# Block-local attention and a noisy top-2 mixture of experts: the rows of x stored once in token order, 16 bytes scattered per token and expert, rows gathered per tile

## The chip, the core and the metric

The kernel runs on one core of a Trainium2 chip. The metric is the device time of one execution in microseconds (us). Five engines work side by side, each through its own instructions in order: TensorE (PE; its weight loads are listed as PEld), VectorE (DVE), ScalarE (ACT), GpSimd (POOL) and SyncE (SP), which here issues plain DMA transfers. POOL issues the indirect ones, whose rows are picked by a list of indices. A wait of one instruction holds up all that stands behind it on the same engine.

## The reference, cut to what matters

```python
# attention in chunks of 64 tokens; q, k, v: (8, 8, 576, 64)
scores = scale * np.matmul(q_c, k_c.transpose(0, 1, 2, 4, 3))
scores = scores - np.max(scores, axis=-1, keepdims=True)
attn = np.exp(scores)
attn = attn / (np.sum(attn, axis=-1, keepdims=True) + 1e-09)
out = np.matmul(attn, v_c)
...
x = attn_out.transpose(0, 2, 1, 3).reshape(B * S, H * D)      # 4608 tokens x 512
noisy_logits = x @ w_gate + np.log1p(np.exp(x @ w_noise)) * noise
top2 = np.argpartition(-noisy_logits, 2, axis=1)[:, :2]       # 2 of 8 experts
...
    h = np.maximum(x[mask] @ w1[e], 0.0)                      # 512 -> 1024
    out[mask] += top2_w[mask, k, None] * (h @ w2[e])          # 1024 -> 512
```

Every token goes through small attention blocks, then through the two experts with the largest noisy logits, and the two results are added with softmax weights.

## The kernel before, in words

**Attention** (`attend`, L593) takes 36 tiles of 128 tokens, one tile a call, as a pipeline over several calls. In call `it` PE makes the scores of tile `it` (L355), the product with v of tile `it-2` (L381), four transposes of the probabilities of tile `it-1` (L371), four transposes of x of tile `it-3` (L396) and the gate logits of tile `it-4` (L409). A product of q and k covers 64 rows of depth for each of two heads: k is kept with zeros in the other head's rows (`KB`, L308), so that 128 rows and 64 columns of the array give the scores of two heads in one matmul of 128 columns; v is kept likewise (`VB`, L309). So a tile's k and v come as two half transfers of 64 partitions each, q as one whole (L317 to L327): five transfers of SP a tile. The scores of tile t lie in PSUM bank t % 2. DVE takes a row maximum (L359), subtracts it (L364), adds 1e-9 to the row sums (L385), takes reciprocals (L388) and writes x (L391); ACT does the exponential and copies out of PSUM.

**Routing** (`route`, L413) goes over six groups of 4 or 8 tiles (L141). It is a generator whose small DVE steps are put between those of attention (`step_route`), and gives each token two slots: a slot belongs to an expert and a place in its list. **Scatter** (L521): for each tile and each of the two choices, POOL copies one number into `spacer` (L528, L530; that paces it by mx, rc or hh) and issues an indirect DMA (L532) which writes 128 rows of 515 numbers, x and three words on token and weights, into the DRAM table `slots`. 72 of these are spread over attention and the first expert block.

**The experts** are taken in 24 blocks of up to 448 rows, three blocks an expert, expert 0 first and the others in the order of their load (L129). A block's first layer is 8 steps f of 12 matmuls, its second 3 or 4 tiles k of 8 steps f of 3 matmuls; every product is split into three of high and low parts (`three`, L256). Blocks 0, 1 and 2 are expert 0. Their rows are loaded by plain transfers out of `slots` (L202) and turned by PE (L246); blocks 0 and 1 are loaded as soon as routing groups 2 and 4 have been scattered (`EARLY`, L137). Later blocks are loaded from `slots` by four transfers a tile (L207), whose rows the chip picks by the expert's number in a register of SP, and turned by DVE (L250). `x_tile` (L237) turns one tile; its place in the order is written out by hand (`TURNS`, L665, and `hook1`, `hook2_f`). `resolve` (L175) makes row numbers and weights of the words in `slots`. The results are added into `out` by indirect DMAs of POOL (L230). `out` is cleared by 37 transfers of SP (L591) while block 0 runs.

The order of all instructions is the order of the code; nothing is rearranged.

Of the kernel before, what the change touches and what calls it, by code (L numbers as in the profile page):

```python
# [19 lines left out]
P = 128  # L20
# [13 lines left out]
ROW = 576  # L34
CODE, WA, WB, USED = DM, DM + 1, DM + 2, DM + 3
CLEAN = max(CAPS) - P
# [17 lines left out]
def kernel(ctx, tc, qT, kT, vh, wgn, noise, w1, w2, out, caps=CAPS):  # L54
# [36 lines left out]
    nc.vector.memset(caprow[:, 0:1], float(caps[0]))  # L91
    run8 = consts.tile([P, NE], FT, name="run8")
# [44 lines left out]
    EARLY = {0: 2, 1: 4}  # L137
# [58 lines left out]
    def gather_tile(i, k):  # L196
        e, b = BL[i]
        j, r = blocks[e][b][k]
        n = rot["xg"] = rot["xg"] + (i >= NPE)
        x = XG[e, j] = (later_xg[0] if n % 8 in (1, 2, 3) and i >= NPE else xg).tile([P, DM], FT, name="xg")  # L200
        if i < NPE:
            d = nc.sync.dma_start(x[0:r], by_slot[j * P:j * P + r, 0, 0:DM])  # L202
            if i in EARLY:
                early_loads.append(d)
            return
        for q in range(4):
            nc.sync.dma_start(x[32 * q:32 * q + 32, 0:4 * r].rearrange("p (t c) -> p t c", c=P),  # L207
                              by_slot[j * P:j * P + r, ds(place[e], 1), q * P:(q + 1) * P]
                              .rearrange("(t p) o c -> p t (o c)", p=32))

    def gather(i):
        for k in range(len(blocks[BL[i][0]][BL[i][1]])):
            gather_tile(i, k)


    later = [(i, k) for i in range(4, NBL) for k in range(len(blocks[BL[i][0]][BL[i][1]]))]

    ahead = [len(blocks[1][0])]

    def gather_more(most):  # L220
        for _ in range(most):
            if later and ahead[0] < LEAD:
                gather_tile(*later.pop(0))
                ahead[0] += 1
# [40 lines left out]
    def layer1(i, hook, hook_d=lambda f, d: None):  # L265
        e, b = BL[i]
        n = sum(r for _, r in blocks[e][b])
        HT[i] = BH[0 if i == 1 else i % 2]
# [32 lines left out]
    last_rows = ExitStack()  # L301
    rows = last_rows.enter_context(tc.tile_pool(name="rows", bufs=5, side="right"))
    gx = pa.enter_context(tc.tile_pool(name="gx", bufs=2, side="right"))
    work = pv_pools.enter_context(tc.tile_pool(name="work", bufs=3, side="right"))
    vs = pv_pools.enter_context(tc.tile_pool(name="vs", bufs=1, side="right"))
    loads = pk.enter_context(tc.tile_pool(name="loads", bufs=1))
    RING = 6
    KB = [loads.tile([P, 2, 4, P], FT, name=f"kb{n}") for n in range(RING)]  # L308
    VB = [vs.tile([P, 2, 2, 4, 65], FT, name=f"vb{n}") for n in range(RING)]  # L309
    QB = {}  # L310
    HALF = (slice(0, 64), slice(64, 128))
    for n in range(RING):
        for t in (KB[n], VB[n]):
            for h in range(2):
                (nc.vector if n < 2 else nc.gpsimd).memset(t[HALF[1 - h], h], 0.0)

    def load_qk(t):  # L317
        if t < NT:
            QB[t] = loads.tile([P, 4, P], FT, name="qb", bufs=RING)
            nc.sync.dma_start(QB[t], qT[:, t])  # L320
            for h in range(2):
                nc.sync.dma_start(KB[t % RING][HALF[h], h], kT[HALF[h], t])  # L322

    def load_v(t):
        if t < NT:
            for h in range(2):
                nc.sync.dma_start(VB[t % RING][HALF[h], h], vh[HALF[h], t])  # L327

    nc.scalar.preload_act_table_set("natural_log_exp_and_others")
    for j in range(5):  # L330
        load_qk(j)
        if j:
            load_v(j - 1)
# [5 lines left out]
    zero = consts.tile([P, USED], FT, name="zero")  # L339
    nc.gpsimd.memset(zero, 0.0)  # L340

    PR, PT, XS, XT, RC = {}, {}, {}, {}, {}
    by_head = lambda a: a.rearrange("p (g k) -> p g k", k=64)
    sco = [by_head(PS[:, b, :]) for b in range(2)]

    def x_at(t):
        u, r = divmod(t, 4)
        if r == 0:
            XS[u] = rows.tile([P, 4, 520], FT, name="xs")
        return XS[u][:, r]  # L350

    def scores(t):
        for hp in range(4):
            for s in HALF:
                nc.tensor.matmul(PS[s, t % 2, hp * P:(hp + 1) * P], QB[t][:, hp, s], KB[t % RING][:, :, hp, s], start=True, stop=True)  # L355

    def soft_max(t):
        mx = work.tile([P, 8], FT, name="mx", bufs=2)
        nc.vector.tensor_reduce(mx, sco[t % 2], AX.X, OP.max)  # L359
        return mx  # L360

    def soft_sub(t, mx):
        PR[t] = work.tile([P, 512], FT, name="pr")
        nc.vector.tensor_tensor(by_head(PR[t]), sco[t % 2], mx[:, :, None].to_broadcast([P, 8, 64]), OP.subtract)  # L364
# [12 lines left out]
    def pv(t):  # L377
        for hp in range(4):
            for c, s in enumerate(HALF):
                o = 130 * (hp % 2)  # L380
                nc.tensor.matmul(PS[s, 3 + hp // 2, o:o + 130], PT[t][:, hp, s], VB[t % RING][:, :, c, hp, :], start=True, stop=True)  # L381
# [8 lines left out]
    def norm_c(t):  # L390
        nc.vector.tensor_tensor(x_at(t)[:, 0:DM].rearrange("p (b g k) -> p b g k", b=2, k=64), pvb[:, :, :, 0:64], RC[t].to_broadcast([P, 2, 4, 64]), OP.mult)  # L391
# [6 lines left out]
    def x_copy(t):  # L398
        XT[t] = gx.tile([P, ND, P], FT, name="xt")
        nc.scalar.activation(XT[t].rearrange("p d n -> p (d n)"), PS[:, 5, :], AF.Copy)  # L400

    def lg_at(t, n=1):
# [485 lines left out]
```

## Time and profile before

| what | before |
|---|---|
| median of 3 runs | 1029.89 us (1028.78 to 1033.22) |
| the profiled execution | 1029.36 us |
| its span, first to last instruction | 1027.6 us |
| PE busy | 983.1 us (96%) |
| DVE, ACT, POOL busy | 446.1, 271.3, 227.4 us |
| mean granted clock of PE | 0.991 |
| DMA traffic | 132.93 MB, mean 129 GB/s |

The span is what the trace covers; the profiled execution's time is 1.8 us longer. "Busy" counts the time in which at least one instruction of the engine ran. A DMA share of 1.0 means that all 16 DMA engines of the core were busy; it is worked out from packets and comes out slightly above 1 where they overlap. Line numbers L... are those of the kernel before.

### The profile page before, as it was taken

To read this page: it belongs to the slowest core of one execution; us is meant where nothing else is said; L and a number is where in the kernel's file an instruction comes from. 1 tells how busy PE (TensorE), PEld (TensorE's weight loads), DVE (VectorE), ACT (ScalarE), POOL (GpSimd) and SP (SyncE) were. 2 spreads that over 40 slices of the span, in tenths; PEclk is the share of its full clock that TensorE was granted. 3 is DMA by queue.
4 is the path that set the end of the run, shared out by engine and by line. 5 is a ranking of instruction groups with operands and counts; after the bars stand their busy time and mean duration, and the time that the engine had idled before them with its cause. 6 is when DMAs were issued, how large, how long until landed. Compare 5 with 4: busy or idle time off the path is not lost.

```text
span 1027.6 us, 16132 instructions
## 1 busy us (share of the span) xinstructions
PE 983.1 (96%) x5962; PEld 883.5 (86%) x5962; DVE 446.1 (43%) x1005; ACT 271.3 (26%) x542; POOL 227.4 (22%) x332
## 2 busy tenths in 40 slices
PE   6889998999799999999999999999999999999996
PEld 6778887898689889888988998899889998999884
DVE  6656665522525443344334432453245324533311
ACT  3434443211314121222222321232123212322100
POOL 3034754751020111111111102101211111101112
PEclk9999999999899999999999999999999999999998
DMA  8899999864561552264225422553244324412213
GB/s 226 259 292 298 328 323 396 310 177 121 88 166 56 124 117 37 60 140 116 40 46 138 124 40 44 125 135 59 36 121 123 74 43 126 120 21 32 31 21 43
DMA packets 103218, 132.93 MB, mean 129 GB/s; under 512 B 22848, under 2 KB 56000, under 8 KB 103136
## 3 DMA queue, kind: packets, MB, share of 16 engines
q1 hardware_dynamic: 86704, 93.54, 30.4%
q0 software_dynamic: 16432, 38.33, 19.1%
q8 instruction: 48, 0.79, 0.3%
q14 instruction: 34, 0.28, 0.1%
HBM read 81.69 MB, written 50.13 MB: 128 GB/s over the span
## 4 chain that ended last, share of the span: by engine, by line
PE 84%; SPq 6%; DMA 5%; DVE 2%; issue 2%; ACT 1%; POOL 0%; DVEq 0%; ACTq 0%; POOLq 0%
PE PS L263 78%; DMA kb<-in_kT 2%; PE PS L381 2%; SPq L322 1%; PE PS L355 1%; SPq L327 1%; DMA xg<-slots 1%; DMA vb<-in_vh 1%; SPq L207 1%; PE PS L409 1%; PE PS L371 1%; SPq L320 1%; DMA out<-zero 1%; PE PS L396 1%; SPq L107 0%
## 5 line engine op out<-in xcount | busy, mean ns | idle before, releaser
L263 PE MATMUL PS<-xh,w1h 128*128 128x384 f32 (+2 forms) x768 | 262.6, 342 | 9.4 <-DVE hl L277 6.2
L230 POOL DMA_INDIRECT out<-o,lid x77 | 119.3, 1549 | 684.5 <-DVE o L283 680.3
L263 PE MATMUL PS<-xh,w1l 128*128 128x384 f32 (+2 forms) x768 | 261.7, 341 | 0.0
L263 PE MATMUL PS<-xl,w1h 128*128 128x384 f32 (+2 forms) x768 | 261.6, 341 | 0.0
L263 PE MATMUL PS<-w2h,hh 128*128 128x512 f32 x616 | 240.5, 390 | 0.0
L263 PE MATMUL PS<-w2h,hl 128*128 128x512 f32 x616 | 240.2, 390 | 0.0
L263 PE MATMUL PS<-w2l,hh 128*128 128x512 f32 x616 | 240.2, 390 | 0.0
L276 ACT ACTIVATE hh<-PS 128x384 fp32r<-128x384 f32 (+2 forms) x192 | 95.0, 496 | 481.0 <-PE PS L263 425.4
L277 DVE SCALAR_TENSOR_TENSOR hl<-PS,hh 128x384 fp32r<-128x384 f32 (+2 forms) x192 | 108.5, 566 | 188.4 <-ACT hh L276 185.5
L283 DVE TENSOR_SCALAR o<-PS,lwt 128x512 f32<-128x512 f32 x77 | 57.7, 749 | 248.6 <-PE PS L263 246.2
L263 PEld LDWEIGHTS PS<-xh,w1h 128*128 128x128 f32 x768 | 145.3, 189 | 12.7 <-DVE hl L277 6.6
L263 PEld LDWEIGHTS PS<-xl,w1h 128*128 128x128 f32 x768 | 145.4, 189 | 1.9
L263 PEld LDWEIGHTS PS<-xh,w1l 128*128 128x128 f32 x768 | 145.2, 189 | 1.1
L263 PEld LDWEIGHTS PS<-w2h,hl 128*128 128x128 f32 x616 | 112.9, 183 | 27.2
L263 PEld LDWEIGHTS PS<-w2l,hh 128*128 128x128 f32 x616 | 112.9, 183 | 26.2
L263 PEld LDWEIGHTS PS<-w2h,hh 128*128 128x128 f32 x616 | 112.9, 183 | 25.8
L532 POOL DMA_INDIRECT slots<-xs,lii x72 | 72.5, 1007 | 26.5 <-issue 20.8
L253 ACT ACTIVATE xh<-y 128x512 fp32r<-128x512 f32 x67 | 41.2, 614 | 105.5 <-DVE y L250 105.5
L254 DVE TENSOR_TENSOR xl<-y,xh 128x512 fp32r<-128x512 f32 x67 | 44.9, 670 | 47.9 <-ACT xh L253 47.2
L355 PE MATMUL PS<-kb,qb 128*64 128x128 f32 x576 | 40.9, 285 | 13.3 <-DMA kb<-in_kT 12.6
L250 DVE STREAM_TRANSPOSE y<-xg 128x512 f32<-128x512 f32 x67 | 45.6, 681 | 11.9 <-DMA xg<-slots 11.9
L381 PE MATMUL PS<-vb,pts 128*64 128x130 f32 x576 | 39.8, 278 | 9.3 <-ACT xt L400 5.6
(114 smaller groups left out, 686.7 us busy)
## 6 DMA issues: line engine op xcount, KB each, us to landing
st<-in_w SPq DMA_DIRECT2D x64, 512.0 KB
xg<-slots SPq DMA_DIRECT2D x252, 64.0 KB
out<-zero SPq DMA_DIRECT2D x37, 256.0 KB
vb<-in_vh SPq DMA_DIRECT2D x72, 130.0 KB
qb<-in_qT SPq DMA_DIRECT2D x36, 256.0 KB
kb<-in_kT SPq DMA_DIRECT2D x72, 128.0 KB
xg<-slots SPq DMA_DIRECT2D x9, 256.0 KB
slots<-zero SPq DMA_DIRECT2D x8, 257.5 KB
```

The lines of the kernel that those rows point to most:

```text
L207: nc.sync.dma_start(x[32 * q:32 * q + 32, 0:4 * r].rearrange("p (t c) -> p t c", c=P), by_slot[j * P:j * P + r, ds(place[e], 1), q * P:(q ...
L230: s = nc.gpsimd.indirect_dma_start(out=out, out_offset=bass.IndirectOffsetOnAxis(ap=rows_of(i, j)[0:r], axis=0), in_=o[0:r], in_offset=Non ...
L250: nc.vector.transpose(y[:, 0:4 * r], x[:, 0:4 * r])
L253: nc.scalar.activation(oh, src, AF.Copy)
L254: nc.vector.tensor_sub(ol, src, oh.bitcast(FT))
L263: nc.tensor.matmul(p, a, b, start=first and n == 0, stop=last and n == 2)
L276: nc.scalar.activation(hh[:, 0:n], p, AF.Relu)
L277: nc.vector.scalar_tensor_tensor(hl[:, 0:n], p, 0.0, hh[:, 0:n].bitcast(FT), op0=OP.max, op1=OP.subtract)
L283: nc.vector.tensor_scalar(o[0:r], p[0:r], weights_of(i, j)[0:r], None, op0=OP.mult)
L355: nc.tensor.matmul(PS[s, t % 2, hp * P:(hp + 1) * P], QB[t][:, hp, s], KB[t % RING][:, :, hp, s], start=True, stop=True)
L381: nc.tensor.matmul(PS[s, 3 + hp // 2, o:o + 130], PT[t][:, hp, s], VB[t % RING][:, :, c, hp, :], start=True, stop=True)
L532: s = nc.gpsimd.indirect_dma_start(out=slots, out_offset=bass.IndirectOffsetOnAxis(ap=lii[:, k, t0 + r:t0 + r + 1], axis=0), in_=XS[(t0 + ...
```

## The change

x is written once, in token order, to a DRAM table `xbuf`: one plain transfer of SP for each 4 tiles. The scatter writes only 16 bytes per token and choice (`mt`: token and expert code, two weights) into `slots`, still by 72 indirect DMAs of 128 rows. For a tile of an expert's list POOL now gathers 128 rows of `xbuf` by an indirect DMA, after `resolve` has made their numbers: for blocks 0 to 2 straight into the tile that PE turns; for later blocks into a buffer `xr`, from which SP writes the tile to DRAM (`save`) and then loads it with the same four transfers as before (`load_tile`). Rows are fetched 6 tiles and loaded up to 7 tiles ahead. Block 2 becomes an early block too, bound to routing group 5, the last. The zeros that were written to `slots` are fewer.

Attention loads q, k and v as whole transfers of 128 partitions for two tiles at a time, 18 of each. The zero halves are gone: scores and the product with v are matmuls on quarters of the array (64 rows and 64 columns), 16 of each a tile in place of 8, each with half the columns. The scores of a tile take half of two PSUM banks, the same two for every tile, where two tiles took turns. The gate logits are made for 4 tiles at a time: 4 matmuls of 512 columns on column strips of 32, a copy (`gate_copy`), and a sum over the strips one call later (`gate_sum`), so that routing of a group starts one call later and the pipeline has one more call at its end.

The core of the diff:

```diff
-    slots = dram.tile([LROWS * NE, ROW], FT, name="slots")
+    xbuf = dram.tile([NROWS, DM], FT, name="xbuf")
+    slots = dram.tile([LROWS * NE, 4], FT, name="slots")
+    sorted_x = [[dram.tile([P, DM], FT, name=f"x{e}_{j}") for j in range(NLIST)] for e in range(NE)]
-    EARLY = {0: 2, 1: 4}
+    FETCH = 6
+    EARLY = {0: 2, 1: 4, 2: 5}
+    def save(keep=0):
+        while len(unsaved) > keep:
+            e, j, r, x = unsaved.pop(0)
+            nc.sync.dma_start(sorted_x[e][j][0:r], x[0:r])
+    def fetch_tile(i, k):
+        save(1)
...
+            nc.gpsimd.indirect_dma_start(
+                out=x[0:r], out_offset=None, in_=xbuf,
+                in_offset=bass.IndirectOffsetOnAxis(ap=rows_of(i, j)[0:r], axis=0))
+            unsaved.append((e, j, r, x))
+    def load_k(j):
+        kb[j] = loads.tile([P, 2, 4, P], FT, name="kb")
+        nc.sync.dma_start(kb[j], kT[:, 2 * j:2 * j + 2])
     def scores(t):
         for hp in range(4):
-            for s in HALF:
-                nc.tensor.matmul(PS[s, t % 2, hp * P:(hp + 1) * P], QB[t][:, hp, s], KB[t % RING][:, :, hp, s], start=True, stop=True)
+            for h, c in HC:
+                r, s = slice(h * 64, h * 64 + 64), slice(c * 64, c * 64 + 64)
+                o = 64 * hp
+                nc.tensor.matmul(PS[s, h, o:o + 64], q[r, t % 2, hp, s], k[r, t % 2, hp, s], start=True, stop=True)
-                in_=XS[(t0 + r) // 4][:, r % 4, 0:USED], in_offset=None)
+                in_=mt[:, t0 + r, :], in_offset=None)
+                    waiting.append((i, turn[0] + 2))
+    def finish_waiting():
+        while waiting:
+            i = waiting.pop(0)[0]
+            resolve_early(i)
+            gather(i)
+            if (it - 2) % 4 == 3:
+                u = (it - 2) // 4
+                nc.sync.dma_start(xbuf[P + 4 * u * P:P + (4 * u + 4) * P].rearrange("(a p) c -> p a c", p=P), XS[u])
+            if i == 1 and f == 2:
+                finish_waiting()                       # layer 1 of block 1
+            if i == 0 and (k, f) == (0, 4):
+                finish_waiting()                       # layer 2 of block 0
-            if f % 2 == 0:
+            if f % 3:
                 scatter(1)
+            if i == 1 and (k, f) == (0, 5):
+                resolve_all()
+                while len(to_fetch) > len(later) - FETCH:
+                    fetch_tile(*to_fetch.pop(0))
+                gather_more(1)
```

How it moves instructions, at three places. First PE in attention, one call of `attend` before (out<-in, then the size of what is written):

```order
L355 MATMUL PS<-kb_142,qb 64x128 x8
L381 MATMUL PS<-vb_146,pts 64x130 x8
L371 MATMUL PS<-ident,pr 128x128 x4
L396 MATMUL PS<-ident,xs 128x128 x4
L409 MATMUL PS<-wg,xt 128x16 x4
```

and two calls of the change, the second and third after a fourth tile:

```order
L384 MATMUL PS<-kb,qp 64x64 x16
L411 MATMUL PS<-vb,pts 64x65 x16
L400 MATMUL PS<-ident,pr 128x128 x4
L439 MATMUL PS<-xt,wg 32x512 x4
L427 MATMUL PS<-ident,xs 128x128 x4
L452 MATMUL PS<-sel,ls 128x16 x4
```

These are the kinds of rows; the first three and L427 stand in every call, L439 in one call of four and L452 in the next one. The counts of scores and of products with v have doubled with half the columns, and the gate's four matmuls a tile have become eight for four tiles.

Second, POOL at the start of block 0's second layer, where L530 and L528 each stand ahead of a scatter (L532). Before, the kinds of rows there are

```order
L530 COPY spacer<-hh_2258 1x1
L532 DMA slots<-xs,lii 44032x576
L528 MEMSET spacer 1x1
L229 MEMSET spacer 1x1
L230 DMA out<-o,lid_111 4736x512
```

with 16 scatters behind hh in block 0's first layer, 4 behind a memset, then the first store into `out`. In the change they are

```order
L569 COPY spacer<-hh_2696 1x1
L571 DMA slots<-mt,lii 44032x4
L567 MEMSET spacer 1x1
L212 MEMSET spacer 1x1
L216 DMA xg<-xbuf,lid_197 128x512
L257 MEMSET spacer 1x1
L258 DMA out<-o,lid_196 4736x512
```

with 16 scatters behind hh, 2 behind a memset, then the three gathers of block 1 (L212 and L216), three scatters, the first store, five scatters, the second store, the last four scatters, the third store, and then the gathers of block 2. Before, block 1's rows were loaded by SP; now they stand behind 18 scatters on POOL.

Third, DVE in block 1's first layer. Before, eight steps hl follow each other. In the change the last three of these rows, the first of nine that make row numbers for block 2, stand behind the third of them (meta_207 is what SP has loaded of block 2's 16-byte entries):

```order
L305 SCALAR_TENSOR_TENSOR hl_3097<-PS,hh_3096 128x384
L305 SCALAR_TENSOR_TENSOR hl_3099<-PS,hh_3098 128x384
L188 TENSOR_SCALAR rsa<-meta_207 128x4
L189 TENSOR_SCALAR rsb<-meta_207 128x4
L593 TENSOR_SCALAR rsk<-slot_157,lim_204 128x4
```

So the steps hl from the fourth on now stand behind a DMA that itself waits for the last scatter.

More of the change, by code (lines that the diff above doesn't have):

```diff
@@ L194 @@
     early_loads = []
-    def gather_tile(i, k):
+    unsaved = []
+    def save(keep=0):
[4 more added lines that the diff above has]
+        save(1)
         e, b = BL[i]
         j, r = blocks[e][b][k]
-        n = rot["xg"] = rot["xg"] + (i >= NPE)
-        x = XG[e, j] = (later_xg[0] if n % 8 in (1, 2, 3) and i >= NPE else xg).tile([P, DM], FT, name="xg")
+        nc.gpsimd.memset(spacer, 0.0)
@@ L201, in gather_tile @@
         if i < NPE:
[L202 to L205, printed above, removed]
+            last = sum(groups[EARLY[i]])
+            x = XG[e, j] = xg.tile([P, DM], FT, name="xg")
+            nc.gpsimd.indirect_dma_start(
+                out=x[0:r], out_offset=None, in_=xbuf[0:P + last * P, :],
+                in_offset=bass.IndirectOffsetOnAxis(ap=rows_of(i, j)[0:r], axis=0))
+        else:
+            x = later_xg[1].tile([P, DM], FT, name="xr")
+            nc.gpsimd.indirect_dma_start(
+                out=x[0:r], out_offset=None, in_=xbuf,
+                in_offset=bass.IndirectOffsetOnAxis(ap=rows_of(i, j)[0:r], axis=0))
+            unsaved.append((e, j, r, x))
@@ L211, in gather @@
     def gather(i):
         for k in range(len(blocks[BL[i][0]][BL[i][1]])):
-            gather_tile(i, k)
-    later = [(i, k) for i in range(4, NBL) for k in range(len(blocks[BL[i][0]][BL[i][1]]))]
-    ahead = [len(blocks[1][0])]
+            fetch_tile(i, k)
+    later = [(i, k) for i in range(NPE, NBL) for k in range(len(blocks[BL[i][0]][BL[i][1]]))]
+    to_fetch = list(later)
+    ahead = [0]
     def gather_more(most):
+        save()
         for _ in range(most):
+            if to_fetch and len(later) - len(to_fetch) < FETCH:
+                fetch_tile(*to_fetch.pop(0))
@@ L337 @@
     nc.sync.dma_start(nz, noise)
-    zero = consts.tile([P, USED], FT, name="zero")
+    zero = consts.tile([P, DM], FT, name="zero")
     nc.gpsimd.memset(zero, 0.0)
+    mt = consts.tile([P, NT, 4], FT, name="mt")
+    nc.gpsimd.memset(mt, 0.0)
+    load_q(3)
+    load_k(3)
+    load_v(3)
     PR, PT, XS, XT, RC = {}, {}, {}, {}, {}
-    by_head = lambda a: a.rearrange("p (g k) -> p g k", k=64)
-    sco = [by_head(PS[:, b, :]) for b in range(2)]
+    sco = PS[:, 0:2, 0:256].rearrange("p h (g k) -> p h g k", k=64)
+    by_head = lambda a: a.rearrange("p (g h k) -> p h g k", g=4, h=2)
+    HC = [(h, c) for h in range(2) for c in range(2)]
     def x_at(t):
@@ L377, in pv @@
     def pv(t):
+        v = vb[t // 2]
         for hp in range(4):
[L379 to L381 removed]
+            for h, c in HC:
+                r, s = slice(h * 64, h * 64 + 64), slice(c * 64, c * 64 + 64)
+                nc.tensor.matmul(PS[s, 3 + h, hp * 65:hp * 65 + 65], PT[t][r, hp, s], v[r, t % 2, c, hp, :],
+                                 start=True, stop=True)
     def norm_a(t):
@@ L426, in route @@
         ts = slice(t0, t0 + G)
-        parts = [(XS[t0 // 4 + a], slice(4 * a, 4 * a + 4)) for a in range(G // 4)]
         nc.scalar.activation(y, lg[:, :, 1, :], AF.Abs)
@@ L594, in attend @@
         STEPS = 2
-        if it > 0:
-            load_qk(it + 4)
-            load_v(it + 3)
-        if it in (5, 7):
-            for r in range(CLEAN + 64 * (it // 2 - 2), CLEAN + 64 * (it // 2 - 1), 16):
-                nc.sync.dma_start(slots[r * NE:(r + 16) * NE, 0:USED], zero)
-        if it == 7:
-            nc.sync.dma_start(slots[(CLEAN + P) * NE:NLIST * P * NE, CODE:USED].rearrange("(p r) c -> p r c", p=P),
-                              zero[:, 0:3 * (NLIST * P - CLEAN - P) // 16].rearrange("p (r c) -> p r c", c=3))
+        if it % 2 == 0 and it >= 2 and it // 2 + 3 < NT // 2:
+            load_q(it // 2 + 3)
+            load_k(it // 2 + 3)
+        if it % 2 == 1 and it >= 3 and (it - 3) // 2 + 4 < NT // 2:
+            load_v((it - 3) // 2 + 4)
+        if it == 5:
+            nc.sync.dma_start(slots[0:NLIST * P * NE].rearrange("(p r) c -> p (r c)", p=P), zero[:, 0:NLIST * NE * 4])
+            nc.sync.dma_start(xbuf[0:P], zero)
+        turn[0] = it
+        if waiting and it >= waiting[0][1]:
+            finish_waiting()
         if it in (12, 14, 16, 18):
@@ L665 @@
     TURNS = (((1, 1), (1, 5), (2, 1)), ((0, 6), (1, 2), (1, 6), (2, 2)))
-    tail = [NT + 2 + a for a in range(2)]
+    tail = [NT + 2 + a for a in range(3)]
     def hook_tail(f, d):
```

167 lines of the change are left out of this document (87 added, 80 removed).

## Prediction

> **What bounds the kernel now.** I read the windows first, one row for each stage, because the shares of the whole span mix attention with the experts. The columns are the length, the busy time of PE, its weight loads, DVE, ACT and POOL with the instructions in brackets, then PE's granted clock, the DMA share and GB/s.
>
> ```profile
> core 0: us, PE busy (x) PEld busy (x) DVE busy (x) ACT busy (x) POOL busy (x), PEclk, DMA share, GB/s
> 0.00:158.00 158.00, 135.27 (x1678) 123.66 (x1678) 102.65 (x371) 66.56 (x141) 66.75 (x115) 0.99 0.94 289
> 51.00:87.00 36.00, 31.59 (x397) 28.98 (x399) 21.79 (x84) 13.29 (x29) 9.91 (x18) 1.00 0.98 282
> 87.00:124.00 37.00, 32.38 (x393) 29.55 (x389) 25.62 (x103) 18.98 (x44) 26.46 (x38) 0.95 1.03 326
> 154.00:184.00 30.00, 24.30 (x210) 22.42 (x209) 17.77 (x88) 12.58 (x28) 15.15 (x25) 1.00 1.05 396
> 266.00:1018.00 752.00, 751.37 (x3744) 672.89 (x3744) 302.18 (x498) 180.03 (x350) 110.98 (x140) 1.00 0.38 82
> ```
>
> From 266 to 1018 us PE is busy for 751.37 of 752 us. Nothing the change does to x can shorten that stretch: its matmuls stay. What can be won lies ahead of 266 us. In attention (to 158 us) the DMA share is 0.94 and PE is busy for 135 of 158 us; neither is full by itself, so the next view is the chain that ended last, in attention's middle:
>
> ```profile
> 66.69 7.50 DMA kb<-in_kT
> 74.19 0.91 issue
> 75.09 1.09 PE PS L355 x16
> 76.19 0.89 PE PS L381 x16
> 77.07 0.58 PE PS L371 x4
> 77.66 0.44 PE PS L396 x4
> 78.09 0.80 PE PS L409 x8
> 79.12 1.02 PE PS L355 x16
> ```
>
> The chain is a load of k for 7.50 us, then some calls of `attend` at PE's own pace: 1.09 + 0.89 + 0.58 + 0.44 + 0.80 = 3.80 us of matmuls a tile. The real pace comes from PE's timeline, by the first scores and those of the last tile, number 35:
>
> ```profile
> 5.52 3.43 PE L355 MATMUL PS<-kb,qb 128*64 128x128 f32 x32 [5.52 <-DMA kb<-in_kT]
> ...
> 154.00 1.09 PE L355 MATMUL PS<-kb,qb 128*64 128x128 f32 x16
> ```
>
> (154.00 - 5.52) / 35 = 4.24 us a tile, 0.44 above PE's. So attention is bound by transfers that come late, with PE close behind. To gain much, the change has to relieve both, and it does touch both.
>
> **Attention, PE.** A chain row counts 16 instructions for 8 matmuls. L396's four take 0.44 us on the whole array, 110 ns for 128 columns; L381's sixteen, also of 128 columns and on half the array, take 0.89 us, 56 ns each. So two halves already run side by side. Quarters of half the columns would be four abreast at 55 ns, eight groups a phase: 0.45 us for each of scores and product with v, if that goes on. L409's eight instructions take 100 ns each for only 16 columns, so a matmul can have a floor near 0.10 us; with that floor for each group of four a phase takes 0.80. The gate costs 0.11 (four strips abreast, 512 columns at the rate of L396) to 0.44 (one after the other), plus 0.10 for a quarter of the sums: 0.2 to 0.55 a tile, I take 0.5. Scores take 1.02 where the product with v takes 0.89; half of that difference stays, 0.08 with rounding. PE then needs 0.53 + 0.45 + 0.58 + 0.44 + 0.5 = 2.5 us a tile, or 3.2 with the floor. TensorEngine Tiling (Array Packing) of the Trainium skill, under Instruction Overhead, speaks against the change: each matmul carries about 60 cycles, and a factor should not be taken from a dimension already small; L409's row agrees that short ones don't scale, and by an estimate of 25 ns a matmul 32 of them take 0.8 us a phase. Both values lie below the DMA's, next, so this choice doesn't move the sum.
>
> **Attention, DVE.** It is busy for 102.65 us over 36 tiles, 2.85 us each. All scores now use the same banks, so a tile's scores wait for the subtraction (L364) of the tile before: two passes over 512 columns behind 0.53 us of scores, about 2.1 us, which hides under the DMA's pace. If transfers became free, DVE would end the last scores at 5.5 + 36 x 2.85 = 108 us.
>
> **Attention, bytes.** The sizes of the transfers and the count of the scatters in attention:
>
> ```profile
> vb<-in_vh SPq DMA_DIRECT2D x72, 130.0 KB
> qb<-in_qT SPq DMA_DIRECT2D x36, 256.0 KB
> kb<-in_kT SPq DMA_DIRECT2D x72, 128.0 KB
> ...
> slots<-zero SPq DMA_DIRECT2D x8, 257.5 KB
> ...
> L530 POOL COPY spacer<-rc 1x1 f32<-1x1 f32 x23 | 4.1, 178 | 43.0 <-DVE rc L388 39.9 <-issue 1.1 <-DVE goh L458 0.9
> L530 POOL COPY spacer<-mx 1x1 f32<-1x1 f32 x21 | 3.7, 178 | 29.8 <-DVE mx L359 24.5 <-DVE gsp L444 4.1 <-DVE goh L458 0.6
> ```
>
> The first window moved 158 x 289 = 45.7 MB. Loads of q, k, v are 36 x 772 KB = 28.5 MB and stay. The 23 + 21 = 44 scatters of 128 rows of 515 numbers are 11.6 MB and go, the zeros of `slots` are 2.1 MB and nearly go; the plain stores of x come in their place, some 8 MB by the last scores. That leaves 45.7 - 11.6 - 2.1 + 8 = 40 MB. At 282 GB/s (51 to 87 us, loads for the most part) they take 142 us, at 326 (87 to 124, many scatters) 123 us, at 396 (154 to 184, mostly writes) 101 us. The mix after the change lies between the first two windows; I take their mean, 304, which gives 132 us, and shave it to 130 for half as many, longer transfers. Last scores at 130 instead of 154: **-24 us**, between -12 (142) and -44 (110, DVE's bound). DMA: Bandwidth & Descriptors of the Trainium skill, under its rules for kernel authors, says that transfers to disjoint partition halves share the same 16 engines, so whole ones would carry no more bytes a second; DMA shares of 0.98 and 1.03 with halves agree, and by it the time is that of the first bound or my value without the shaving. SP issues three transfers for two tiles where it issued ten; that is slack on SP, not time. The tail from the last scores to the experts keeps its work; the call more and the gate's later sum replace other steps there: 0, within 2.
>
> **Block 1's rows, behind POOL.** PE's timeline at the start of block 0's second layer and of block 1's first:
>
> ```profile
> 192.39 0.39 PE L263 MATMUL PS<-w2h,hh 128*128 128x512 f32 x1
> 192.62 0.40 PE L263 MATMUL PS<-w2l,hh 128*128 128x512 f32 x1
> ...
> 210.20 0.33 PE L263 MATMUL PS<-xh,w1h 128*128 128x384 f32 x1
> ```
>
> POOL's timeline around the start of that layer:
>
> ```profile
> 190.67 0.99 POOL L532 DMA_INDIRECT slots<-xs,lii  x1 [0.16 <-issue]
> ...
> 196.84 0.98 POOL L532 DMA_INDIRECT slots<-xs,lii  x1 [0.16 <-issue]
> 197.82 0.09 POOL L528 MEMSET spacer<- 1x1 f32 x1
> 198.12 0.97 POOL L532 DMA_INDIRECT slots<-xs,lii  x1 [0.22 <-issue]
> 199.09 0.09 POOL L528 MEMSET spacer<- 1x1 f32 x1
> ```
>
> and SP's load of block 1, released by the scatter of 190.67:
>
> ```profile
> 193.45 1.36 SPq L202 DMA_DIRECT2D xg<-slots  x3
> ```
>
> POOL does a scatter in 1.27 us (197.82 to 199.09), and that is the time of its instruction, not of its bytes: I keep it for 16 bytes and for a gather. Its 16th scatter behind hh ends at 197.82, 5.4 us after the second layer begins. Two more scatters (2.6), the first gather (1.3) and a landing (that scatter ended at 191.66, SP went on at 193.45: 1.8) put the first rows 11.1 us into that layer. PE is to turn them after ten steps of three matmuls at 0.23 us, 6.9 us in. PE stands for 4.2 us, and a little more as the other two gathers follow at 1.3 us: **+5**. Were a gather cheaper than a scatter or POOL's queue empty earlier, 0; with slower gathers 9.
>
> **Block 2's numbers, in front of hl.** In block 1's first layer DVE waits, behind the third hl, for the words of the last scatter. On POOL after the 18th scatter (8.0 us into block 0's second layer) come 3 gathers, 12 scatters and two stores, the store's price being
>
> ```profile
> L230 POOL DMA_INDIRECT out<-o,lid x77 | 119.3, 1549 | 684.5 <-DVE o L283 680.3
> L229 POOL MEMSET spacer<- 1x1 f32 x77 | 45.6, 592 | 0.0
> ```
>
> 1.549 + 0.592 = 2.14 us: 8.0 + 15 x 1.3 + 2 x 2.14 = 31.8, and 4 us more to land and load. DVE is there at 17.8 (192.39 to 210.20) + 5 (the wait above) + three steps of 12 x 0.17 = 2.1 us: 29. It stands 7 us, and hl of the next steps and the turned tiles of block 2 queue behind it; PE has free banks for two to three steps, some 5 us, less what DVE then must catch up: **+4**, from 0 (POOL ahead of time) to 10.
>
> **The start of later tiles.** DVE waits 11.92 us for the first later tile and PE 6.18:
>
> ```profile
> 263.50 0.71 DVE L250 STREAM_TRANSPOSE y<-xg 128x512 f32<-128x512 f32 x1 [11.92 <-DMA xg<-slots]
> 266.19 0.74 PE L263 MATMUL PS<-xh,w1h 128*128 128x448 f32 x1 [6.18 <-DVE hl L277]
> ```
>
> This wait goes, since block 2's rows and numbers come earlier and block 3's tiles are fetched from block 1 on. But a chain of six gathers through three buffers, saves and loads is what is late next; its first tile costs about a gather, a landing, a save and a load, some 8 us at 2 us each, and six of them are hidden only if POOL is not behind. -6 + 2 = **-4**, from -6 to +2.
>
> **The rest.** From 266 us fewer gathers than the 77 stores of L230, at 1.3 us, bring POOL from 111 to at most 211 of 752 us. Saves and gathers add at most 77 x 2 x 256 KB = 40 MB to 62 MB, a share of 0.38 to about 0.63. `save` waits on SP for a gather, and weights and tile loads queue behind it; tiles come up to 7 ahead, some 40 us of matmuls, which hides it: 0. With that cover gone, each late tile would cost PE some 2 us.
>
> Sum: -24 + 5 + 4 - 4 = -19. The profiled execution took 1029.36 us, 0.5 below the median of the runs; 1029.4 - 19 = **1010 us**.
>
> **The rivals.** *Quarters one after the other.* If four quarter matmuls don't overlap, a phase is 32 x 56 ns = 1.78 us, PE needs 1.86 + 1.78 + 0.58 + 0.44 + 0.5 = 5.2 us a tile, the last scores are at 5.5 + 35 x 5.2 = 187, 33 later than now: 1029 + 33 + 5 = 1067. It decides from 1.3 us a phase on, where PE is slower than now. The halves that overlap today speak against it, L409's floor speaks for it: 0.07. *No gain in transfer rate, and POOL's chain twice as dear.* Last scores at 142 (-12) and +18 - 4: about 1031, no change; the milder form, -12 with my other terms, gives 1022. The share of 0.98 at 282 GB/s speaks for it; against it, that the second window did more. Chance 0.18, two thirds of it at 1022. *Transfers faster.* With fewer, longer ones at 396 GB/s DVE bounds, last scores at 110 (-44): 990. Mostly writes ran at that rate, so 0.13. *The change doesn't do what it says*, x still arriving late because POOL sets all: part of the second. The forecast itself keeps 0.62.
>
> **How the numbers follow.** A change of 0.5%, 5 us, is about what a measurement of this kernel can tell from none. 990 and 1022 belong in the range, 1067 does not: low 988, high 1024, which leaves out some 0.2. Faster by over 0.5%: the forecast, the fast case and two thirds of the second, 0.86; same 0.06; slower 0.08.
>
> **What would show it.** In the profile after: scores of tile 35 near 130 us and a DMA share near 1 until then; 0.45 to 0.8 us of L384 and of L411 a tile; PE's idle time before block 1's turned rows of about 5 us, released by a gather; DVE's idle before the first row numbers of block 2, about 7 us; no stretch of idle PE over 1 us after block 3 starts. It is wrong if the last scores lie after 145 us, if L384 takes over 1.3 us a tile, or if PE stands in the later blocks.

## The result, and the profile after

The change makes the kernel slower: 1054.55 us (median of 4 runs, 1052.50 to 1056.94) against 1029.93 (4 runs), a ratio of 1.0235 with a 95% interval of 1.0200 to 1.0269. The forecast was 1010, from 988 to 1024. The profiled execution took 1052.5 us with a span of 1050.5. In the table the forecast is the moment before plus the forecast's terms up to it.

| moment, us from the span's start | before | after | forecast for after |
|---|---|---|---|
| first scores of tile 35 | 154.0 | 156.9 | 130 |
| first layer of block 0 | 167.3 | 169.0 | 143 |
| second layer of block 0 | 192.4 | 191.7 | 168 |
| start of the unbroken run of 3744 matmuls | 266.2 | 285.7 | 247 |
| last matmul | 1017.6 | 1037.1 | 999 |
| end of the span | 1027.6 | 1050.5 | 1009 |

The windows of the kernel after, with the columns and most of the stretches shown of before:

```profile
core 0: us, PE busy (x) PEld busy (x) DVE busy (x) ACT busy (x) POOL busy (x), PEclk, DMA share, GB/s
0.00:158.00 158.00, 119.70 (x2620) 96.02 (x2620) 98.25 (x358) 70.48 (x147) 59.02 (x101) 0.87 0.76 272
51.00:87.00 36.00, 29.93 (x657) 24.34 (x656) 22.54 (x85) 15.86 (x36) 10.31 (x17) 0.86 0.90 322
87.00:124.00 37.00, 27.72 (x586) 21.81 (x585) 26.04 (x103) 20.54 (x45) 26.24 (x36) 0.86 0.66 232
154.00:184.00 30.00, 25.21 (x294) 21.59 (x294) 18.20 (x77) 13.42 (x30) 15.52 (x26) 0.94 0.61 212
```

The DMA share of attention falls from 0.94 to 0.76, and from 1.03 to 0.66 between 87 and 124 us: the transfers no longer bind. But PE is not busier for it, it is busy for 119.7 us instead of 135.3, and its granted clock falls from 0.99 to 0.87. Something other than transfers now sets (156.94 - 6.13) / 35 = 4.31 us a tile (here the first and the last two tiles):

```profile
6.13 1.13 PE L384 MATMUL PS<-kb,qp 64*64 64x64 f32 x32 [6.13 <-DMA kb<-in_kT]
...
148.84 0.69 PE L384 MATMUL PS<-kb,qp 64*64 64x64 f32 x32 [1.52 <-DVE pr L393]
...
156.94 0.87 PE L384 MATMUL PS<-kb,qp 64*64 64x64 f32 x24
```

From 7 to 157 us PE is busy for 117.8 us, 3.4 a tile, and idle for 32.2, 0.9 a tile. The largest of its waits there (us in total, times, longest):

```profile
PE PS L411 <- issue: 13.1, 25, 1.3
PE PS L411 <- DVE gsp L482: 7.6, 5, 1.8
PE PS L384 <- DVE pr L393: 5.0, 6, 1.5
```

No wait for a load is left; before, they made 7.1 of 16.7 idle us from 7 to 154 us, and "issue" 0.8. One call of `attend` on PE's timeline shows what a quarter phase looks like:

```profile
51.72 0.69 PE L384 MATMUL PS<-kb,qp 64*64 64x64 f32 x32
52.24 0.58 PE L411 MATMUL PS<-vb,pts 64*64 64x65 f32 x8
53.22 0.36 PE L411 MATMUL PS<-vb,pts 64*64 64x65 f32 x6 [0.41 <-issue]
53.97 0.55 PE L411 MATMUL PS<-vb,pts 64*64 64x65 f32 x18 [0.38 <-issue]
54.45 0.66 PE L400 MATMUL PS<-ident,pr 128*128 128x128 f32 x4
```

and POOL's timeline beside it:

```profile
51.16 1.01 POOL L571 DMA_INDIRECT slots<-mt,lii  x1 [0.54 <-issue]
...
52.50 0.98 POOL L571 DMA_INDIRECT slots<-mt,lii  x1 [0.16 <-issue]
```

The 32 instructions of the scores take 0.5 us, as hoped. Those of the product with v stop after 8 and again after 6, with "issue" as the reason: PE waits for nothing that the profile shows. Counted by the starts of neighbouring matmuls of one line, there are 24 such pauses of over 0.5 us between 10 and 158 us (most of 0.60 to 0.68), and none before. Of the 24, 21 overlap a scatter or gather of POOL, as the two here do, though these fill only 27% of that time.

The call from tile 34's scores to tile 35's is a special one. It takes 8.1 us (148.84 to 156.94) where before took 3.8 (150.23 to 154.00): POOL sends three gathers and two scatters in a row until 153.16, the product with v stops twice for 1.3 to 1.4 us, and DVE's row maximum starts at 154.26 although the scores were over at 149.53. One call earlier the change was still 1.4 us ahead of before.

Behind attention, three waits of PE answer to the forecast's. First, block 1's rows. The chain of waits:

```profile
198.08 2.43 DMA meta<-slots
200.51 0.68 issue
202.36 3.41 DMA xg<-xbuf,lid
205.81 1.11 PE PS L274 x4
```

and POOL's and PE's timelines there:

```profile
200.03 0.09 POOL L212 MEMSET spacer<- 1x1 f32 x1
202.36 0.98 POOL L216 DMA_INDIRECT xg<-xbuf,lid  x1 [2.23 <-DVE rsk L594]
```

```profile
205.81 0.47 PE L274 MATMUL PS<-ident,xg 128*128 128x128 f32 x1 [7.09 <-DMA xg<-xbuf,lid]
```

PE stands for 7.09 us. POOL is through its 18 scatters at 200.03, as counted, then waits 2.23 us for the row numbers, whose words SP asked for at 198.08, behind 37 clearings of `out` that occupy it from 168.75:

```profile
168.75 29.23 SPq L636 DMA_DIRECT2D out<-zero  x37
```

Second, block 1's first layer. PE's and ACT's timelines:

```profile
220.15 0.33 PE L291 MATMUL PS<-xh,w1l 128*128 128x384 f32 x1
...
229.39 0.69 PE L291 MATMUL PS<-xh,w1h 128*128 128x384 f32 x1 [3.79 <-DVE hl L305]
```

```profile
228.25 0.49 ACT L304 ACTIVATE hh<-PS 128x384 fp32r<-128x384 f32 x1 [11.03 <-remote]
```

PE stands for 3.79 us because hh and hl are late; but PE's first step was over at 220.5, and hh did not start before 228.25. In the trace's semaphore events, PE's signals after 216.6 are recorded at 228.18, 228.30 and 228.43, while its steps ended at 220.5, 222.6 and 225.6. POOL sent scatters and stores one after the other until 227.0. DVE's numbers for block 2 came after that and held nobody up.

Third, the first later tiles. The chain:

```profile
254.41 15.24 DMA x<-xr
269.79 0.95 POOL xr L221
...
272.30 4.38 DMA xr<-xbuf,lid
...
278.90 4.05 DMA xg<-x
282.97 0.72 DVE y L278
...
285.72 751.36 PE PS L291 x3744
```

A save of 256 KB takes 15.24 us to land, a fourth gather waits for its buffer, the loads for the saves, and PE stands for 11.14 us before 285.72 (6.18 before). From there both kernels are alike: 751.4 us for 3744 matmuls. At the end the span reaches 13.4 us past the last matmul instead of 10.0; the longest of POOL's closing drains, the last column of min/median/max in ns, after and then before:

```profile
L949 POOLq DRAIN  x3: 46/107/6930, 1042.8 to 1050.3; - x3
```

```profile
L884 POOLq DRAIN  x3: 46/107/4235, 1022.5 to 1027.3; - x3
```

### The profile page after: what moved, and what is told of

Read it like the earlier page. It is cut to its first block, busy times and chain, and to the rows that moved or that the text cites. A ratio compares the mean times of both kernels' runs of the same rounds, so it can differ in the third digit from the quotient of the medians.

```text
span 1050.5 us, 17698 instructions
## 1 busy us (share of the span) xinstructions
PE 970.6 (92%) x6970; PEld 855.6 (81%) x6970; DVE 443.9 (42%) x1001; ACT 276.5 (26%) x551; POOL 303.4 (29%) x471
## 4 chain that ended last, share of the span: by engine, by line
PE 84%; DMA 3%; DVE 3%; SPq 3%; issue 2%; another core or an unknown queue 2%; ACT 2%; POOL 0%; ACTq 0%; DVEq 0%; POOLq 0%
PE PS L291 74%; SPq L636 3%; PE PS L411 3%; PE PS L384 2%; PE PS L400 2%; DMA x<-xr 1%; PE PS L427 1%; PE PS L439 1%; DVE mx L388 1%; PE PS L452 1%; DVE pr L393 1%; DMA kb<-in_kT 0%; PE PS L274 0%; DMA xr<-xbuf,lid 0%
## 5 line engine op out<-in xcount | busy, mean ns | idle before, releaser
L221 POOL DMA_INDIRECT xr<-xbuf,lid x67 | 66.8, 997 | 134.4 <-DMA x<-xr 114.7
L571 POOL DMA_INDIRECT slots<-mt,lii x72 | 71.9, 998 | 20.9 <-issue 20.2
L411 PE MATMUL PS<-vb,pts 64*64 64x65 f32 x1152 | 36.3, 244 | 26.0 <-issue 13.6
L411 PEld LDWEIGHTS PS<-vb,pts 64*64 64x64 f32 x1152 | 29.2, 152 | 31.8 <-issue 18.2
```

Of the source, the lines that this page charges most:

```text
L221: nc.gpsimd.indirect_dma_start(out=x[0:r], out_offset=None, in_=xbuf, in_offset=bass.IndirectOffsetOnAxis(ap=rows_of(i, j)[0:r], axis=0))
L411: nc.tensor.matmul(PS[s, 3 + h, hp * 65:hp * 65 + 65], PT[t][r, hp, s], v[r, t % 2, c, hp, :], start=True, stop=True)
L571: s = nc.gpsimd.indirect_dma_start(out=slots, out_offset=bass.IndirectOffsetOnAxis(ap=lii[:, k, t0 + r:t0 + r + 1], axis=0), in_=mt[:, t0 ...
```

## The experiments

**Which part of attention?** Four kernels undo or take one part. "Last scores" is the start of tile 35's scores.

```diff
 e1: scores on halves, as before                    e2: bank 0 for every tile
-    nc.tensor.matmul(PS[s, h, o:o + 64], q[r, t % 2, hp, s], k[r, t % 2, hp, s], ...)
+    nc.tensor.matmul(PS[s, t % 2, hp * P:(hp + 1) * P], QB[t][:, hp, s], KB[t % RING][:, :, hp, s], ...)
```

> The change with one part undone: scores and product with v on halves of the array with zero halves in k and v, half loads, one score bank a tile in turn, as before; 16-byte scatters, stores of x, the gate by fours stay. In the change tile 35's scores come at 157.0 us with a mean clock of 0.87 in attention. Theory (the quarters made PE's share so thin that its clock is halved again and again, and one pair of score banks ties PE to DVE): clock 0.97 or more, about 3.9 us a tile, last scores at 143 to 147, time about 1042. Rival (the transfers still set the pace): last scores at 152 to 156 with a DMA share over 0.9. Rival (another part of the change, the scatter or the gate by fours, slows attention): last scores at 155 to 160, DMA share under 0.8.

Measured: 1059.83 us, 1.0278 of before (1.0240 to 1.0315). Last scores at 163.8, clock 0.97, DMA share 0.97 and 262 GB/s from 10 to 140 us, no pause. The theory's time failed, the rival of the transfers was nearest and still too early: with half loads attention is bound by DMA, at fewer bytes but also fewer bytes a second than before (292 GB/s there). The last call is special here too: PE stands in it for 8.07 us,

```profile
159.68 2.00 PE L412 MATMUL PS<-vb,pts 128*64 128x130 f32 x16 [8.07 <-ACT xt L433]
```

after DVE waited 5.85 us, until 154.59, for block 0's 16-byte entries; before has no such load in attention. Tile 34's scores came at 150.5, as before (150.2).

> As the kernel with halves, but the scores of every tile go to the same bank, so that a tile's scores wait for the subtraction of the tile before. If the one bank is a cause by itself: last scores at least 10 us later than with halves and two banks. If it is covered, as the prediction had it: within 3 us.

Measured: last scores at 162.9, 1060.56 us, with a like wait of 10.7 us. No cost, but under transfers that bind anyway a bank can't show one; g1 and g2 ask again.

The attention of the change on the kernel before (with its gate and its scatters of 515 numbers):

> The kernel before with only the attention part of the change: whole loads for two tiles and matmuls on quarters with one pair of score banks; gate a tile at a time, scatters of 515 numbers a row, no store of x, the later stages as before. Theory (quarter matmuls pause while POOL sends a scatter, halves do not, and the pauses and thin work let PE's clock fall): pauses over 0.5 us inside the quarter phases once scatters run, clock in attention 0.83 to 0.92, DMA share 0.7 to 0.9, last scores at 152 to 160, no earlier than before (154.0). Rival (the new data path, with 16 bytes a row and stores of 1 MB, is what spoils attention): clock 0.95 or more, last scores at 125 to 140.

Measured: 1029.39 us; last scores at 157.7, 9 pauses. The windows' row for attention:

```profile
0.00:158.00 158.00, 129.85 (x2740) 121.42 (x2744) 96.42 (x360) 65.91 (x140) 58.52 (x98) 0.86 0.84 301
```

As the theory had it: transfers relieved, clock down, nothing gained, and 8 of the 9 pauses overlap a scatter. The new data path is not needed to spoil attention.

No scatter until the calls of `attend` are issued:

```diff
-            scatter(1, mx[0:1, 0, 0:1])
+    scatter(len(pending))          # behind the loop over the 36 calls
```

> The change without any scatter during the 36 calls of attend; those that have gathered are issued in a row behind them, so block 0's rows are late and the whole time is some 40 to 70 us longer: only attention is compared. If the stalls inside the products with v and the late maxima (some 20 us) come with POOL's scatters: last scores at 135 to 147 instead of 157.0. If they come from the quarter matmuls or from the instruction stream: 153 to 158.

Measured: 1101.29 us, last scores at 192.6; neither case. Until 117 us POOL sent nothing: tile 28 came at 114.3 instead of 120.9, and there were still 7 pauses. So pauses don't need scatters. These seven, of 0.7 to 3.1 us, are of another kind, though: each begins within 2 us of the start of a 16 KB transfer of the DMA queue "q8 instruction", of which 16 lie in that stretch. (Their number goes with that of PE's instructions: in the first 158 us 13 before, 20 in the change. That PE waits for them is not shown.) Then POOL sent its scatters in a row, and PE all but stopped; the windows' row from 127 to 150 us and PE's timeline in it:

```profile
127.00:150.00 23.00, 5.76 (x24) 3.22 (x24) 1.06 (x3) 0.00 (x0) 19.05 (x37) 0.50 0.03 2
```

```profile
139.07 0.26 PE L384 MATMUL PS<-kb,qp 64*64 64x64 f32 x1 [1.74 <-issue]
139.78 0.35 PE L384 MATMUL PS<-kb,qp 64*64 64x64 f32 x1 [0.46 <-issue]
```

The same on halves:

> The kernel with halves, with no scatter in attention; POOL sends 40 to 60 of them in a row while the last calls of attend still run, so attention and the whole are some 40 us longer or not by what happens there, and the end of attention alone is compared with the like kernel with quarters, where PE started one quarter matmul in 0.7 to 2.8 us from 127 to 171 us. Theory (only quarters are held up by POOL): in the row of scatters halves run on at 56 ns each, last scores at 150 to 165. Rival (any matmul of attention is held up): calls of over 20 us there, last scores after 185.

Measured: 1109.06 us, last scores at 200.2; halves started one matmul in 0.7 to 2.8 us too, and so did transposes on the whole array. My theory fell: a row of scatters holds up any matmul of attention.

**The clock.** Four matmuls more in each call, whose result nothing reads:

```diff
+            for hp in range(4):
+                nc.tensor.matmul(PS[:, 2, hp * P:(hp + 1) * P], ident, ident, start=True, stop=True)
             pv(it - 2)
```

> The change with four more matmuls of 128 columns on the whole array in each call of attend, ahead of the product with v, whose result nothing reads: 16 us more work for PE over attention. Theory (what is lost is the clock, which is halved in 41 of 158 us because PE does too little): clock in attention from 0.87 to 0.95 or more, last scores at 148 to 155 instead of 157.0 although PE has more to do. Rival (the clock follows the waiting and does not cause it, PE's pace is set by DVE and the pauses): clock up, last scores at 157 to 165. If the filler does not count for the clock: 0.87 as now and 165 or later.

Measured: 1058.50 us, last scores at 160.3. The windows' row:

```profile
0.00:158.00 158.00, 135.82 (x2832) 112.25 (x2832) 98.18 (x350) 68.63 (x143) 56.71 (x97) 0.99 0.75 267
```

The clock is back at 0.99 and nothing is won: the last scores come 3.3 us later, as the rival had it. But the filler is more than I took: its four matmuls are eight instructions in a call, and these take 39.2 us of PE in all, not 16. The group, and one call of it behind a phase of quarters:

```profile
L659 PE MATMUL PS<-ident 128*128 128x128 f32 x264 | 39.2, 292 | 0.1
```

```profile
72.58 0.69 PE L384 MATMUL PS<-kb,qp 64*64 64x64 f32 x32
73.21 1.16 PE L659 MATMUL PS<-ident 128*128 128x128 f32 x8
```

At this clock the 32 instructions take 0.63 us (the median of both phases here); in the change the medians are 0.91 and 1.02. The pauses are 10 instead of 24, all beside a scatter or gather. So the clock and PE's idle time paid for nearly all of the filler, and what a full clock would be worth without it this run can't tell. That a full clock is not enough by itself is shown by g3, below: 0.98, and last scores at 160.7.

**Loads, banks, instructions.** These use the whole loads on halves of the array. Without zero halves each score sums two heads, so the attention is not the reference's, and the loop for rows beyond the lists is left out: only the pace of attention is read.

```diff
 g1 (g2: bank 0 for every tile)
+    nc.tensor.matmul(PS[s, t % 2, hp * P:(hp + 1) * P], qp[t // 2][:, t % 2, hp, s], kb[t // 2][:, t % 2, hp, :], ...)
 g3: as g2, each matmul in two of half the columns
+    for a in range(2):
+        nc.tensor.matmul(PS[s, 0, o:o + 64], qp[t // 2][:, t % 2, hp, s], kb[t // 2][:, t % 2, hp, 64 * a:64 * a + 64], ...)
```

> The change with matmuls on halves of the array again, two score banks in turn, but its whole loads: k and v have no zero halves, so each score is the sum over two heads and the attention is not the reference's; the loop for rows beyond the lists is left out. Only the pace of attention is read. PE needs about 3.8 us a tile, transfers are the change's. Theory (in the change one pair of banks ties PE and DVE together, so that their waits add up; quarters have room for no second pair): with two banks PE's pace holds, last scores at 138 to 146. Rival (pauses, POOL's scatters and routing set the pace whatever the array): 150 to 160.

> The same with one score bank for all tiles; everything else, the sums over two heads too, as there. Theory (the one bank ties PE and DVE together): at least 8 us later than with two banks, last scores at 150 to 165. Rival (the quarters themselves, their instructions and thin work, are what costs): within 4 us of the kernel with two banks, and both under 146.

> The kernel with halves on whole loads and one bank (sums over two heads, so not the reference's attention; its last scores came at 144.8), with each of its matmuls of scores and of products with v cut into two of half the columns: as many instructions as with quarters, on halves of the array. If the pauses of the quarters come from the number of instructions: pauses over 0.5 us inside these phases, ten or more of them, last scores at 152 to 162. If they come from the quarter form itself: no or hardly any pauses, last scores at 144 to 150.

Measured: last scores at 140.8 (g1), 144.8 (g2) and 160.7 (g3), with 0, 0 and 11 pauses. For g2 and then g3, the groups of PE in attention: instructions, busy us, mean ns, idle time before them and its reasons:

```profile
L383 PE MATMUL PS<-kb,qp 128*64 128x128 f32 x576 | 42.1, 291 | 11.5 <-DMA kb<-in_kT 6.0 <-DVE pr L392 5.5
L409 PE MATMUL PS<-vb,pts 128*64 128x130 f32 x576 | 40.4, 282 | 10.6 <-DVE gsp L479 6.3 <-ACT gex L506 2.0 <-ACT xt L430 2.0
```

```profile
L412 PE MATMUL PS<-vb,pts 128*64 128x65 f32 x1053 | 45.4, 227 | 16.0 <-issue 7.8 <-DVE gsp L482 4.7 <-ACT gex L509 2.4
L385 PE MATMUL PS<-kb,qp 128*64 128x64 f32 x1120 | 43.6, 232 | 10.1 <-DMA kb<-in_kT 6.0 <-DVE pr L394 4.1
```

Two banks are worth 4 us. Twice the instructions, at the same area and columns, cost 16 and bring the pauses ("issue 7.8") back: these come with the number of instructions, not with the quarter form. The eleven pauses sum to 7.5 us between starts; the two phases are also longer without a pause, by 0.05 and 0.08 us a call (medians), and the last call takes 8.4 us instead of 4.3. Ten of the eleven overlap a scatter or gather. g1 and g2 send the same scatters with half as many matmuls and have no pause, so a scatter alone does not make one.

**Why the loads are faster.** Half loads for two tiles at a time:

```diff
-            nc.sync.dma_start(KB[t % RING][HALF[h], h], kT[HALF[h], t])
+            nc.sync.dma_start(KB[j % RING][HALF[h], h], kT[HALF[h], 2 * j:2 * j + 2])
```

> The kernel with halves, half loads and two score banks on the change's data path (last scores at 163.8 with a load a tile; 140.8 on whole loads), with each half load fetching two tiles, 4 KB a partition in a row, and q for two tiles in one load. If length is what made the change's loads faster: DMA rate in the first 40 us over 350 GB/s instead of 252, last scores at 140 to 148. If it is that they fill 128 partitions: rate under 290, last scores at 156 to 165.

Measured: last scores at 155.0, 1052.90 us, between the two forecasts. The windows' row of the first 40 us for half loads of a tile (e1), half loads of two tiles (e7) and whole loads of two tiles (g1):

```profile
5.00:40.00 35.00, 30.73 (x368) 25.66 (x368) 23.31 (x56) 14.29 (x30) 5.86 (x12) 1.00 0.87 252
```

```profile
5.00:40.00 35.00, 29.19 (x344) 24.68 (x344) 20.84 (x43) 13.38 (x28) 8.79 (x11) 0.95 1.04 272
```

```profile
5.00:40.00 35.00, 31.42 (x392) 26.64 (x394) 23.88 (x68) 15.75 (x33) 0.00 (x0) 1.00 0.96 381
```

With all DMA engines busy, halves of twice the length move 272 GB/s and whole loads 381: the rate comes with the 128 partitions, not with the length. In time the step to pairs counts too: tile 34's scores come at 150.5 (e1), 144.7 (e7) and 136.9 (g1). e7 also holds the loads of 8 tiles where e1 holds 6, so the first 5.8 us need not be the length's.

**The first later tiles.** Expert 1's first weights loaded behind the first saves and tile loads (h1), or each load as four of 32 rows (h2):

```diff
 h1: w_load(1, 1, c) for the four c behind gather_more(1) in block 1's second layer, step (0, 5)
 h2:
+        if which == 1 and e == 1:
+            for j in range(4):
+                nc.sync.dma_start(st[32 * j:32 * j + 32], w1v[ds(place[e], 1), c, j].rearrange("o r f -> (o r) f"))
```

> The change, with the four loads of expert 1's first weights issued behind the first saves and tile loads of block 3 instead of ahead of them. Theory (the saves of the gathered rows stand behind those weights in the DMA queues, 15.2 us for one): the wait of 11.1 us ahead of block 3 falls under 2 us, time about 1044. Rival (six gathers through three buffers set it): 8 us or more remain, time 1051 or more.

Measured: 1053.13 us, 1.0219 of before (1.0176 to 1.0261). The forecast time failed: the wait moved. DVE's timeline has the first tile at 264.37 instead of 282.97, as the theory had it, but stands 24 us for the second, which is now the one behind the weights; PE then stands 15.81 us at 293.63:

```profile
264.37 0.71 DVE L278 STREAM_TRANSPOSE y<-xg 128x512 f32<-128x512 f32 x1 [2.57 <-DMA xg<-x]
...
291.71 0.71 DVE L278 STREAM_TRANSPOSE y<-xg 128x512 f32<-128x512 f32 x1 [24.12 <-DMA xg<-x]
```

> The change with each of the four loads of expert 1's first weights issued as four transfers of 32 rows. Theory (the load as it stands has an outermost dimension of 4 and so uses 4 of the 16 DMA engines, 100 GB/s, for 25 us; on these four everything else of SP's queue, a save of 15.2 us among it, waits): the 4096-byte packets then run on 12 to 16 engines at once and are through in under 10 us, the first tile of block 3 is loaded 10 us earlier, the wait of 11.1 us falls to 0 to 4, time 1043 to 1048. Rival (the chain of six gathers through three buffers sets it): 8 us or more remain.

Measured: 1039.91 us, 1.0121 of before (1.0089 to 1.0153), so 14.6 less than the change, or 11.7 by the two ratios (before took 1028.72 us beside it). PE's wait of 11.1 us is gone. Windows while the weights come in, the change and then h2:

```profile
260.00:266.00 6.00, 6.00 (x31) 5.56 (x31) 1.85 (x3) 1.09 (x2) 0.00 (x0) 1.00 0.26 104
```

```profile
242.00:248.00 6.00, 6.00 (x30) 4.96 (x29) 2.94 (x11) 0.71 (x2) 2.02 (x3) 1.00 0.88 172
```

A DMA share of 0.26 is four engines of sixteen, at 104 GB/s: the load's outermost dimension is 4. The Trainium skill, DMA: Bandwidth & Descriptors, Rules for kernel authors, has this as a rule (an outermost dimension smaller than 16 confines a transfer to at most as many engines), and the trace agrees.

**A faster kernel.** The kernel before had the same jam:

> The kernel before with only the four loads of expert 1's first weights issued as four transfers of 32 rows each. Before, they ran from 234 to 262 us on four DMA engines, and the first later tile, loaded behind them, came late: PE stood 6.2 us at 260. Theory: the wait of 6.2 us falls under 1.5, time 1023 to 1026, faster than both kernels. Rival (the tile waits for the row numbers or the last scatter): 5 us or more remain, time 1028 to 1031.

Measured: 1017.39 us, 0.9907 of before (0.9886 to 0.9929), faster than both kernels; no wait of PE over 1 us is left behind 177 us. The theory held, though the time lies below its range: before took 1026.24 us beside it, and the last scores came 2 us earlier as well, which the theory does not explain.

> The kernel before with two small parts: expert 1's first weights in transfers of 32 rows (alone: 0.9907 of before, last scores at 151.9), and q, k, v loaded for two tiles at a time, k and v still as halves. If longer pieces load faster: last scores at 138 to 146, time 1004 to 1010. If only whole loads do: last scores at 149 to 155, time 1014 to 1019.

Measured: 1017.99 us, 0.9880 (0.9859 to 0.9901), last scores at 152.5, as the second case had it: on halves longer loads add nothing clear.

## Why the prediction was wrong, point by point

**The step that failed: "PE then needs ... 2.5 us a tile, or 3.2 with the floor", with "this choice doesn't move the sum".** Attention was forecast as the slowest of three mean rates (PE 2.5, DVE 2.85, DMA about 3.5 us a tile), with PE's waits for the others put at nothing. PE's tile came out at 4.31 us: 3.4 busy, at a clock of 0.87, and 0.9 idle (13.6 us "issue", 13.0 for DVE, 5.1 for ACT). The transfers were relieved even more than I took: at 381 GB/s the rival of the fast transfers was the right one for them. The changes from e1 to the change can be put in a row by the scores of the last tile, 35, and of the one before it:

| step | last scores, us | worth | tile 34 | worth |
|---|---|---|---|---|
| e1: halves, half loads, two banks | 163.8 | | 150.5 | |
| g1: whole loads | 140.8 | -23.0 | 136.9 | -13.6 |
| g2: one bank | 144.8 | +4.0 | 140.5 | +3.6 |
| g3: as many instructions as with quarters | 160.7 | +15.9 | 152.2 | +11.7 |
| the change: quarters | 156.9 | -3.8 | 148.8 | -3.4 |

(single executions on several chips; the middle three on sums over two heads). The change, h1 and h2, alike in attention, lie at 155.6 to 158.1, so steps of 4 us are not far above what one execution can tell. The last call takes 13.3 us in e1, with its wait for block 0's entries, some 4 in g1 and g2, and over 8 in g3 and the change; so the columns to the right are the fairer ones. Whole loads gave 14 to 23 of the 24 us that the forecast gave to attention. Cutting the matmuls into twice as many gave most of it back, and quarters returned 3.4 to 3.8 us. I had weighed a floor of time per matmul and had it hidden under DMA. At a full clock the phases are close to that forecast (0.63 us each in f1); the cost is of another kind, pauses without a releaser and waits between engines, which mean durations of L396 and L409 can't show. The Trainium skill, TensorEngine Tiling (Array Packing), Instruction Overhead, spoke against the change, and the time agrees; the 0.8 us a phase that I estimated from its 60 cycles is somewhat above the 0.63, and the pauses are not in it.

**One pair of banks**, costed at nothing under the DMA's pace: 4 us, since that cover was gone.

**Whole or half loads.** From the rule of the Trainium skill, DMA: Bandwidth & Descriptors, Rules for kernel authors, that two halves share the same 16 engines, I concluded that whole transfers carry no more bytes a second, which would have given my first bound. The rule doesn't say that; it only advises one transfer of 128 partitions. The measurement, 252 and 272 against 381 GB/s, decides against my conclusion; the DMA shares of 0.98 and 1.03 that I set beside it as agreeing were engines kept busy longer, not engines at their best.

**Block 1's rows** (+5): 7.1. Place and mechanism right; SP's clearings of `out` in front of the word load were not counted.

**Block 2's numbers** (+4): 3.8, but by another mechanism, so the number was luck. DVE did not wait there. PE's signals came late while POOL sent scatters and stores without a break; that the one causes the other is not shown.

**The start of later tiles** (-4): +5, from 6.2 to 11.1. I took a save at 2 us "if POOL is not behind"; one took 15.2 behind weights on four engines, as h1 and h2 show. The wait of 6.18 that I had "going" was this jam, put down to row numbers.

**The rest**: nothing from 266 us on, and the unbroken 751.4 us say the same. I had left out the end: 3.5 us more, with 77 more indirect transfers over the run and a drain of 6.93 instead of 4.24 us on POOL.

**The account**: attention +26 against its forecast at block 0's start (over 4 of them in the last call), block 0's first layer -2.3 (22.7 us instead of 25.1), these waits 2 + 0 + 9, some 4 of matmuls at a lower clock (0.90 instead of 0.99 from block 0's second layer to the unbroken run), the end 3.5: together about 42 of the 42.5 us between 1010 and the profiled execution's 1052.5. The median lies 2 us above that. The rival that ended slower, quarters one after the other, was not it either: four quarters do run abreast (32 instructions in 0.5 us).

## What to carry to other kernels

When one limit goes, the next mean rate is not the time: ask what waits the other engines impose on each other in each call, and count instructions as a cost of their own (here twice as many at equal work cost 12 to 16 us in attention). Before a wait is put down to the data it waits for, look how many DMA engines run in front of it: a share of 0.26 was here a load on four engines, and a save behind it took 15.24 us. Load 128 partitions at once where the matmul allows it (381 against 272 GB/s).

## What was not expected of the hardware

A row of scatters on POOL, 1.27 us each, with the DMA engines nearly idle (share 0.03), brought PE in attention to one matmul in 0.7, 1.4, 2.1 or 2.8 us, on quarters, halves and the whole array alike; 16 scatters in block 0's first layer did nothing of the kind to its matmuls. In the change, single pauses are mostly of 0.6 to 0.7 us or about twice that, and 21 of 24 lie beside a scatter or gather. The seven of e3 without scatters lie by 16 KB instruction transfers instead. That more instructions bring more pauses is shown by g3; what PE waits for in them, and why a row of scatters makes it so much worse, stays open.
